# Reading three quarters of w_in once and copying them on chip, with an earlier request for x's third quarter

## The chip, the cores and the metric

One core of one Trainium2 chip. The metric is the device time of one execution in microseconds (us). Executions of one kernel agree within about 0.3%, so a change of 1 us (0.14%) can be seen only in several rounds beside the kernel before.

## The reference, cut to what matters

A causal depthwise convolution over 7 positions with softmax weights, then a two-layer product with leaky ReLU:

```python
w = softmax(weight)                       # 8 heads x 7
out[b, s, ch] = sum_k w[head(ch), k] * x_pad[b, s + k, ch]   # x: 8 x 4096 x 192
h = out.reshape(32768, 192) @ w_in        # w_in: 192 x 2048
g = maximum(0.01 * h, h)
result = g @ w_out                        # w_out: 2048 x 192
```

## The kernel before

Work runs in groups of two batch rows by 256 or 512 positions. The two rows sit in the two partition halves (0 to 63 and 64 to 127), so each half needs its own copy of w_in. A group of 256 positions has eight *steps*: step u multiplies w_in's columns (PSUM tile `ph`, two buffers; PSUM is the memory that TensorE writes), and ScalarE evicts it, that is, copies it out, through leaky ReLU into `g`. Steps 1 and 2 use the first quarter of w_in's columns, steps 3 and 4 the second quarter, and so on. The second product (`po`) of a group runs a group later, interleaved with the first product of the next. Group 0 has nothing to interleave, so it is the start of the pipeline.

```python
def load_first(q, after=None):            # x of the first two blocks, four quarters, SyncE
    t = stage_pool.tile([128, 2, HS, D], FP32, name="x_nat")     # 2 buffers
    for e in range(2):
        ins = nc.sync.dma_start(out=t[:, e, :, :], in_=x[e, q*HT:(q+1)*HT, :]...)
        if after is not None and e == 0:
            tc.add_manual_dep(ins.ins, after.ins.name, ..., reason="leave the DMA engines to w_in")
...
for q in range(WQ):                       # WQ = 4; both halves are read from memory, cast to bf16
    for e in range(2):
        fs = slice(q * F // WQ, (q + 1) * F // WQ)
        nc.gpsimd.dma_start(out=w_in[e*CH:(e+1)*CH, :, fs], in_=moe_w_in[:, fs]...)
nc.gpsimd.dma_start(out=w_out, in_=moe_w_out...)
...
load_first(2, low)                        # low: a ScalarE instruction of the setup
...                                       # conv of group 0 on TensorE (2 chunks) and VectorE (1)
load_first(3); load_x(2); transpose_x(2)
...
def mm1(grp, u):                          # one step
    ph = psum_h.tile([128, 2, ST], FP32, name="ph", tag="ph")
    ...  for c in range(NCH): for e in range(2):
             nc.tensor.matmul(out=ph[:, e, ...], lhsT=w_in[ps, c, f*128:(f+1)*128], rhs=y[ps, c, ...])
    nc.scalar.activation(out=g[blk][...], in_=ph..., func=Prelu, alpha=0.01)
...
# in group 0 (i == 0), after step u (counted from 0):
#   u == 1: transpose_first(1), evac_first(1) on VectorE
#   u == 2: cast_first(2, e) on ScalarE       u == 4: transpose_first(2); evacs[0](act_scale)
#   u in (3, 5): 28 conv matmuls of group 1 each
#   after u == 7: evac_first(2), four conv steps ("early"), evacs[1], all on VectorE
# in group 1: transpose_first(3), later evac_first(3) on VectorE
```

## Time and profile before

| | before |
|---|---|
| time, median | 698.46 us (698.27 to 698.76) |
| span of the profiled run | 696.4 us |
| TensorE busy, share of the chain | 99%, 97% |
| steady stage (both products alternate) starts | about 24 us |

The steady stage is the same in all kernels here: from one fixed point of it, the start of group 1's steps 7 and 8, to the end there are 664.8 to 665.5 us in each of the traces. So that start time is a ruler for the whole span; I call it the ruler step. In the kernel before it is 31.22 us. The lines below are TensorE's order in time: start, length, line and operation, and in brackets its idle time and who ended it.

```profile
13.14 1.75 PE L356 MATMUL ph<-yt,w_in 64*128 64x256 bf16 x24 [0.28 <-ACT g L363]
14.82 1.72 PE L201 MATMUL acc<-xt,diag 64*64 64x256 bf16 x28
20.90 1.48 PE L356 MATMUL ph<-yt,w_in 64*128 64x256 bf16 x24
31.22 1.49 PE L356 MATMUL ph<-yt,w_in 64*128 64x256 bf16 x24
```

Steps 3 and 4 start at 13.14 us, 28 conv matmuls at 14.82, steps 7 and 8 at 20.90 us, and the ruler step at 31.22.

### The profile page before, as it was taken

The page shows a single profiled execution, that of the slowest core. Times are in us where ns is not written, and L with a number is a line of the kernel's source. Part 1 is how long each engine was busy: PE and PEld are TensorE (multiplying, and loading weights), DVE is VectorE, ACT ScalarE, POOL GpSimd, SP SyncE. Part 2 cuts the span into 40 slices and gives each one's busy share as a digit, 9 for nine tenths or more (in the row PEclk, how much of TensorE's full clock was granted, in tenths as well). Part 3 has the DMA queues.
Part 4 walks back from the last instruction along what each step waited for, and adds up shares of the span by engine and source line. Part 5 has one row for each costly group of instructions (what it writes and reads, how often), then busy time and mean ns, then how long its engine had stood idle before and what let it go on. Part 6 is the DMA issues. An engine that isn't in the chain of part 4 may idle for free.

```text
span 696.4 us, 26058 instructions
## 1 busy us (share of the span) xinstructions
PE 689.5 (99%) x11786; PEld 612.7 (88%) x11786; DVE 538.2 (77%) x991; ACT 513.3 (74%) x579; POOL 142.1 (20%) x198
## 2 busy tenths in 40 slices
PE   8999999999999999999999999999999999999997
PEld 6899999678888888888888888888888888888887
DVE  6899999768777788777787777787777787777712
ACT  6888888977777777777777777777777777777770
POOL 6342221320122220222220222211222220000000
PEclk9999999999999999999999999999999999999999
DMA  9986553853556545556545556645556644122112
GB/s 173 127 98 76 82 80 77 88 78 73 76 65 92 82 70 81 74 66 93 81 69 81 73 69 93 79 67 85 66 76 88 86 71 72 53 52 59 47 37 69
DMA packets 184847, 54.39 MB, mean 78 GB/s; under 512 B 148384, under 2 KB 184736, under 8 KB 184736
## 3 DMA queue, kind: packets, MB, share of 16 engines
q0 software_dynamic: 98768, 14.17, 29.7%
q1 hardware_dynamic: 85968, 38.56, 23.1%
q8 instruction: 92, 1.51, 0.9%
q14 instruction: 19, 0.16, 0.1%
HBM read 29.88 MB, written 25.17 MB: 79 GB/s over the span
## 4 chain that ended last, share of the span: by engine, by line
PE 97%; DMA 1%; ACT 1%; POOL 0%; issue 0%; DVE 0%; SPq 0%; POOLq 0%; ACTq 0%
PE po L376 49%; PE ph L356 47%; DMA x_nat<-in_x_dram 1%; ACT g L363 1%; PE acc L201 0%; PE wps L268 0%; ACT diag L296 0%; POOL sel L228 0%; PE warm L250 0%; PE ptr L143 0%; ACT x_bf L128 0%; ACT xt L157 0%; POOL sel L226 0%; DVE o_sb L415 0%; POOL ident masks.py:199 0%
## 5 line engine op out<-in xcount | busy, mean ns | idle before, releaser
L363 ACT ACTIVATE g<-ph 128x1024 bf16<-128x1024 f32 x512 | 496.5, 1021 | 161.0 <-PE ph L356 161.0
L182 DVE SCALAR_TENSOR_TENSOR yt<-xt,wk,yt 128x512 bf16<-128x512 bf16 (+1 forms) x642 | 439.7, 685 | 17.4
L376 PE MATMUL po<-w_out,g 64*128 64x192 bf16 (+1 forms) x8048 | 398.1, 243 | 0.1
L376 PEld LDWEIGHTS <-g 64*128 64x128 bf16 (+1 forms) x8048 | 372.2, 94 | 28.8 <-ACT g L363 0.4
L356 PE MATMUL ph<-yt,w_in 64*128 64x512 bf16 (+1 forms) x3552 | 391.8, 347 | 1.6 <-ACT g L363 1.3
L356 PEld LDWEIGHTS <-w_in 64*128 64x128 bf16 x3552 | 249.9, 94 | 46.1 <-issue 5.0
L79 POOL DMA_DIRECT2D x_bf<-in_x_dram x180 | 133.7, 773 | 431.0 <-DMA xt<-x_bf 422.9
L415 DVE COPY o_sb<-po 128x192 f32<-128x192 f32 x216 | 77.2, 358 | 129.5 <-PE po L376 127.2
L176 DVE TENSOR_SCALAR yt<-xt,wk 128x512 bf16<-128x512 bf16 (+1 forms) x107 | 35.9, 336 | 1.0 <-DMA xt<-x_bf 0.8
L415 ACT COPY o_sb<-po 128x192 f32<-128x192 f32 x40 | 13.1, 327 | 0.0
L201 PE MATMUL acc<-xt,diag 64*64 64x256 bf16 x112 | 7.3, 280 | 0.0
L201 PEld LDWEIGHTS <-diag 64*64 64x64 bf16 x112 | 6.0, 111 | 1.2 <-issue 0.6
L250 PE MATMUL warm<-zero 128*128 128x256 bf16 x20 | 4.5, 373 | 1.1 <-DVE junk L218 1.1
L128 ACT CAST x_bf<-x_nat 128x384 bf16<-128x384 f32 x5 | 2.5, 507 | 3.6 <-DMA x_nat<-in_x_dram 3.6
L238 POOL DMA_DIRECT2D w_in<-in_moe_w_in_dram x8 | 5.1, 643 | 0.0
L157 DVE COPY xt<-ptr 128x384 bf16<-128x384 bf16 x7 | 2.2, 352 | 2.8 <-PE ptr L143 2.8
L250 PEld LDWEIGHTS <-zero 128*128 128x128 bf16 x20 | 2.0, 122 | 2.2 <-DVE junk L218 1.1
L296 ACT ACTIVATE diag<-ident,wkl 128x64 bf16<-128x64 bf16 x14 | 3.6, 339 | 0.0
L128 DVE CAST x_bf<-x_nat 128x384 bf16<-128x384 f32 x3 | 1.2, 439 | 1.4 <-DMA x_nat<-in_x_dram 1.4
L317 ACT ACTIVATE yt<-acc,rsum 128x256 bf16<-128x256 f32 x3 | 1.4, 470 | 1.2 <-PE acc L201 1.2
L143 PEld LDWEIGHTS <-x_bf 64*128 64x128 bf16 x48 | 1.2, 101 | 1.0 <-ACT x_bf L128 1.0
L268 PEld LDWEIGHTS wps<-w,sel 8*128 8x128 f32 x6 | 1.4, 322 | 0.7 <-POOL sel L228 0.7
(28 smaller groups left out, 12.5 us busy)
## 6 DMA issues: line engine op xcount, KB each, us to landing
out_dram<-o_sb SPq DMA_DIRECT2D x128, 192.0 KB, 2.1
x_bf<-in_x_dram POOLq DMA_DIRECT2D x180, 64.0 KB, 3.3
x_nat<-in_x_dram SPq DMA_DIRECT2D x8, 192.0 KB, 5.8
w_in<-in_moe_w_in_dram POOLq DMA_DIRECT2D x8, 192.0 KB, 7.8
xt<-x_bf SPq DMA_TRANSPOSE x90, 2.5
w_out<-in_moe_w_out_dram POOLq DMA_DIRECT2D x1, 768.0 KB, 14.2
w<-in_weight_dram SPq DMA_DIRECT2D x1, 0.2 KB
```

Of the source, the lines that this page charges most:

```text
L79: nc.gpsimd.dma_start(out=t[:, c, :, e, :], in_=src[2 * rp + e, :, :, c * CH : (c + 1) * CH],)
L128: copy(out=x_bf[q // 2][:, :, h * HS : (h + 1) * HS, e, :], in_=x_nat[q][:, e, :, :].rearrange("p s (c k) -> p c s k", c=NCH),)
L176: lambda s=src, d=dst, c=c: nc.vector.tensor_scalar_mul(d, s, wk[:, c, 0:1])
L182: lambda s=src, d=dst, c=c, k=k: nc.vector.scalar_tensor_tensor(out=d, in0=s, scalar=wk[:, c, k : k + 1], in1=d, op0=mybir.AluOpType.mult, ...
L201: lambda k=k, p=p, a=a, e=e, ps=ps: nc.tensor.matmul(out=acc[ps, :T], lhsT=diag[c][ps, p, k, :], rhs=xt[0][ps, c, a : a + T], start=(k == ...
L238: nc.gpsimd.dma_start(out=w_in[e * CH : (e + 1) * CH, :, fs], in_=moe_w_in[:, fs].rearrange("(c p) f -> p c f", p=CH),)
L250: nc.tensor.matmul(out=wa[:, 0, 0:HT], lhsT=zero[:, 0:128], rhs=zero, start=True, stop=True)
L296: act = nc.scalar.activation(out=diag[c][:, 1, k, :], in_=ident2, func=mybir.ActivationFunctionType.Copy, scale=wkl[:, c, k : k + 1],)
L356: nc.tensor.matmul(out=ph[:, e, i * T : (i + 1) * T], lhsT=w_in[ps, c, f * 128 : (f + 1) * 128], rhs=y[ps, c, t0 : t0 + T], start=(c == 0) ...
L363: act = nc.scalar.activation(out=g[blk][:, nf * u : nf * (u + 1), :, t0 : t0 + T], in_=ph.rearrange("p e (i t) -> p i e t", i=nf), func=my ...
L376: ins = nc.tensor.matmul(out=po[m], lhsT=g[b][ps, fc, e, s * 128 : (s + 1) * 128], rhs=w_out[ps, fc, :], start=(rt != 1 and fc == 0), stop ...
L415: copy(out=o_sb[:, n % 2, :], in_=po.pop(n))
```

## The change

The intent: read w_in's last three quarters once instead of twice, copy them to the other partition half by on-chip transfers, and so free the DMA engines for x's third quarter, which loses its artificial wait. The request for w_out stands in the source after the copies, that of block 2's x inside group 1. Some warm-up matmuls go, and one conv eviction moves from ScalarE to VectorE. The core of the diff, cuts marked:

```diff
-    def load_first(q, after=None):
+    def load_first(q):
...                                     (the manual dependence goes)
-    for q in range(WQ):
-        for e in range(2):
...
-    nc.gpsimd.dma_start(out=w_out, in_=moe_w_out.rearrange("(c p) d -> p c d", p=128))
+    fq = [slice(q * F // WQ, (q + 1) * F // WQ) for q in range(WQ)]
+    for q, e in [(0, 0), (0, 1)] + [(q, 0) for q in range(1, WQ)]:
+        nc.gpsimd.dma_start(
+            out=w_in[e * CH : (e + 1) * CH, :, fq[q]],
+            in_=moe_w_in[:, fq[q]].rearrange("(c p) f -> p c f", p=CH),
+        )
...                                     (wkh and wkl shrink to the chunks that use them)
+    load_first(2)
+    for q in range(1, WQ):
+        nc.sync.dma_start(out=w_in[CH:128, :, fq[q]], in_=w_in[0:CH, :, fq[q]])
+    w_out = const_pool.tile([128, NFC, D], BF16)
+    nc.gpsimd.dma_start(out=w_out, in_=moe_w_out.rearrange("(c p) d -> p c d", p=128))
...
-    load_first(2, low)
...
-        warm(3)                        (after each conv chunk of group 0)
...
-    load_x(2)
-    transpose_x(2)
...
-                    evacs[0](act_scale)
...
+                evacs[0](nc.vector.tensor_scalar_mul)
...
+            if i == 1 and j == 1:
+                load_x(2)
+            if i == 2 and j == 1:
+                transpose_x(2)
```

More of the change, by code (lines that the diff above doesn't have):

```diff
@@ L103, in new_xt @@
         nc.vector.memset(xt[rp][:, :, 0:HALO], 0.0)
-    def load_first(q, after=None):
+    def load_first(q):
         t = stage_pool.tile([128, 2, HS, D], FP32, name="x_nat")
         for e in range(2):
-            ins = nc.sync.dma_start(
+            nc.sync.dma_start(
                 out=t[:, e, :, :],
@@ L113, in load_first @@
             )
-            if after is not None and e == 0:
-                tc.add_manual_dep(
-                    ins.ins, after.ins.name,
-                    mybir.DependencyInfo(
-                        mybir.DependencyClass.Sync, mybir.DependencyReason.DATA
-                    ),
-                    reason="leave the DMA engines to w_in",
-                )
         x_nat[q] = t
@@ L234 @@
     w_in = const_pool.tile([128, NCH, F], BF16)
-    for q in range(WQ):
-        for e in range(2):
-            fs = slice(q * F // WQ, (q + 1) * F // WQ)
-            nc.gpsimd.dma_start(
-                out=w_in[e * CH : (e + 1) * CH, :, fs],
-                in_=moe_w_in[:, fs].rearrange("(c p) f -> p c f", p=CH),
-            )
-    w_out = const_pool.tile([128, NFC, D], BF16)
-    nc.gpsimd.dma_start(out=w_out, in_=moe_w_out.rearrange("(c p) d -> p c d", p=128))
+    fq = [slice(q * F // WQ, (q + 1) * F // WQ) for q in range(WQ)]
[4 more added lines that the diff above has]
+        )
     wa = psum_h.tile([128, 2, ST], FP32, name="warm", tag="ph")
@@ L278 @@
     wraw = wps[:, 0, 0 : NCH * (K + 1)].rearrange("p (c k) -> p c k", c=NCH)
-    wkh = const_pool.tile([128, NCH, K], BF16, name="wkh")
-    wkl = const_pool.tile([128, NCH, K], FP32, name="wkl")
-    nc.vector.tensor_copy(out=wkh, in_=wraw[:, :, 0:K])
-    nc.vector.tensor_sub(wkl, wraw[:, :, 0:K], wkh)
+    wkh = const_pool.tile([128, NPEC, K], BF16, name="wkh")
+    wkl = const_pool.tile([128, NPEC, K], FP32, name="wkl")
+    nc.vector.tensor_copy(out=wkh, in_=wraw[:, 0:NPEC, 0:K])
+    nc.vector.tensor_sub(wkl, wraw[:, 0:NPEC, 0:K], wkh)
+    rsum = const_pool.tile([128, NCH, 1], FP32)
+    wk = const_pool.tile([128, NCH, K], FP32, name="wk")
     diag = [const_pool.tile([128, 2, K, CH], BF16, name=f"diag{c}") for c in range(NPEC)]
@@ L295, in diag_low @@
         for k in ks:
-            act = nc.scalar.activation(
+            nc.scalar.activation(
                 out=diag[c][:, 1, k, :], in_=ident2,
@@ L299, in diag_low @@
             )
-        return act
     transpose_first(0)
@@ L306 @@
     evac_first(0, nc.vector.tensor_copy, nc.scalar.copy)
-    low = diag_low(0, range(2, K))
+    diag_low(0, range(2, K))
     diag_high(1)
     diag_low(1, range(K))
-    rsum = const_pool.tile([128, NCH, 1], FP32)
     nc.vector.tensor_scalar_add(rsum, wraw[:, :, K : K + 1], 1e-9)
     nc.vector.reciprocal(rsum, rsum)
-    wk = const_pool.tile([128, NCH, K], FP32, name="wk")
     nc.vector.tensor_mul(wk, wraw[:, :, 0:K], rsum.to_broadcast([128, NCH, K]))
+    load_first(2)
[3 more added lines that the diff above has]
+    nc.gpsimd.dma_start(out=w_out, in_=moe_w_out.rearrange("(c p) d -> p c d", p=128))
     def act_scale(out, in_, scale):
@@ L328 @@
         evac_y(act_scale)
-        warm(3)
     cast_first(1, 0, nc.vector.tensor_copy)
```

## The prediction

> **What bounds the kernel now.** I read the page first, then the chain of waits over the first 26 us, then the order of instructions on TensorE and ScalarE there, then the DMA queues in short windows. The page says who owns the span:
>
> ```profile
> PE 689.5 (99%) x11786; PEld 612.7 (88%) x11786; DVE 538.2 (77%) x991; ACT 513.3 (74%) x579; POOL 142.1 (20%) x198
> PE 97%; DMA 1%; ACT 1%; POOL 0%; issue 0%; DVE 0%; SPq 0%; POOLq 0%; ACTq 0%
> ```
>
> The chain is 97% TensorE, and the 1% that is DMA (some 7 to 9 us) stands in one place. The chain in order of time shows where:
>
> ```profile
> 8.02 8.96 DMA x_nat<-in_x_dram
> 16.98 0.02 issue
> 17.00 0.51 ACT x_bf L128
> 17.51 0.93 ACT g L363
> 18.44 0.04 issue
> 18.48 0.83 PE ph L356 x12
> 19.32 1.65 PE acc L201 x28
> 20.97 0.78 PE ph L356 x12
> 21.75 0.02 issue
> 21.77 1.95 ACT g L363 x2
> 23.72 0.04 issue
> 23.76 0.83 PE ph L356 x12
> 24.59 1.14 PE po L376 x14
> ```
>
> The third quarter of x (x_nat, requested at 7.61 and 8.02 us) takes 8.96 us to land. ScalarE, which works in order, stands before its cast with the leaky-relu evictions of group 0 behind it, and TensorE runs out of free ph banks. From 24.4 us on both products alternate and TensorE never stops: a step of 24 ph and 32 po matmuls each 2.63 us. The change touches nothing after that except one transpose, so only the time at which that stage begins can move. How much idle time is there to win:
>
> ```profile
> 12.00:24.31 12.31, 10.56 (x189) 8.50 (x185) 9.30 (x23) 9.52 (x12) 4.30 (x7) 1.00 1.53 207
> 24.31:34.70 10.39, 10.39 (x210) 10.14 (x207) 9.75 (x23) 8.40 (x12) 4.84 (x8) 1.00 1.26 87
> ```
>
> After the length, the second number is TensorE: 12.31 - 10.56 = 1.75 us idle before the steady stage, none in it. The most that perfect transfers could give is near 1.75 us, 0.25% of 698.46.
>
> **What the queues look like.** The share of the two queues between 8 and 10 us, and from 10 to 12 us (packets, MB, share of 16 engines):
>
> ```profile
> q0 software_dynamic: 333, 0.32, 107.6%
> q1 hardware_dynamic: 2, 0.00, 0.1%
> ...
> q0 software_dynamic: 387, 0.36, 114.0%
> q1 hardware_dynamic: 38, 0.03, 5.7%
> ```
>
> x_nat was requested at 7.61 us by SyncE on q1, yet q1 moves nothing until about 11.5 us. An output store on idle queues has its first packet 0.89 us after its request and has landed after 2.0 us. So 3 us of the delay come from GpSimd's queue: at 94 ns for one of its 1 KB casting packets that is about 32 packets an engine. I choose the reading that a newly arriving q1 transfer first waits for some 32 packets per engine that q0 has already queued; once running, the two alternate (from 12 to 16 us q0 moves 560 packets, q1 516).
>
> The eight w_in loads, requested from 2.90 to 7.98 us, land one by one at 9.0, 10.1, 11.05, 12.3, 13.7, 15.9, 17.2 and 18.6 us; alone on the engines each takes some 1.1 us. None of them holds TensorE today: the quarters are complete at 10.1, 12.3, 15.9 and 18.6 us and first used at 11.1, 13.1, 16.5 and 20.9 us.
>
> **What the Trainium skill says.** "DMA: Bandwidth & Descriptors", section "Issuing engines are not separate DMA queues": transfers of SyncE, ScalarE and GpSimd run on the same 16 DMA engines and interleave. The trace agrees from 12 us on, but the 3 us of silence at 8.5 to 11.5 us is more than fair interleaving. The same page, section "Two DMAs through the same engine are not ordered": a transfer that reads what another writes must be issued after that one's semaphore; so each copy costs a second full latency in series. "TensorE: Matmul & The Clock Gate", section "What's actually happening": the clock gate closes after an idle window of about 3.4 us; in this trace the granted clock is 1.00 in every window that I read after the start, with no idle stretch near that long.
>
> **The change part by part.**
>
> Removed: three w_in loads of 192 KB through q0 (3 x 1.1 = 3.3 us of DMA time). Added: three copies of 192 KB on q1, 192 packets of 1 KB, 12 an engine; a 768-byte plain packet takes 48 ns, so I estimate 55 to 60 ns, 0.7 us each alone. DMA time saved: about 1.2 us in all, less than the halved reads suggest.
>
> Moved earlier: the third quarter of x loses its artificial wait and is requested when the buffer's second cast ends, at 5.3 instead of 7.6 us. q1 is still running the second quarter then, so it goes on alternating with w_in: 32 packets an engine, some 9 pairs at about 200 ns until 8.5 us (w_in is slow there, 150 ns a packet), the other 23 at 142 ns: 11.8 us, landed near 12.2 instead of 17.0. ScalarE's wait of 1.57 us and what it passes on are gone. In return w_in pays 32 x 48 ns = 1.5 us: the second half of quarter 0 lands at 10.9, the first half of quarter 1 at 12.3 instead of 11.05 us.
>
> Not moved, in spite of its place in the source: w_out and block 2's x. GpSimd's stream holds nothing else that waits, so w_out is requested right behind the fifth w_in load, at about 6.1 us (2.9 + 5 x 0.63), x from 7.3 us on. They stand in q0 when the copies come.
>
> The copies: SyncE can request the first only when its source has landed, 12.3 us. It waits 0.9 us for its first packet, then for up to 32 packets of q0 (4 of w_in at 95 ns, 28 of w_out at 51 ns: 1.8 us), runs 12 packets alternating with w_out (12 x 0.108 = 1.3 us), and needs 0.4 us to report: 16.6 us. Without the queueing, 14.8 us; unloaded, 14.3 us. The others follow some 1 to 1.5 us apart. So the second half of quarter 1, today there at 12.3 us, becomes the last to arrive. I take 16.0 us.
>
> TensorE from there: group 0's third and fourth ph steps (1.4), 28 conv matmuls (1.72), a step (0.7), 12 transposes (0.36), a step (0.7), 28 conv matmuls (1.65) come to 6.5 us until the seventh step, which today starts at 20.9 us. Break-even is thus a third step at 14.4 us. At 16.0 us the steady stage begins 1.6 us late; every us of start is a us of end.
>
> Small things: two groups of three warm matmuls go (2 x 0.5 us), but the first ph step still needs VectorE's own conv chunk, ended at 10.79 us, and w_in at 10.9, against a start at 11.11: 0.2 us at most, swallowed by the wait that follows. One ScalarE eviction (0.48 us) becomes a VectorE one (0.48 us). Smaller wkh and wkl: nothing. Sum: +1.6 us, less a little for the chance that I see the queue too dark: 698.46 + 1.4 = 699.9 us.
>
> **The rivals.** (1) The intended gain: copies land soon, x_nat no longer stalls, the third step starts at 13.1 to 13.5 us. Then -1 to -1.5 us, 697.0 to 697.5. For it: ScalarE's wait is real and the page shows the DMA engines full. Against: the source lands no earlier than 11.05 us and an idle-queue transfer takes 2.0 us. (2) Copies wait longer: SyncE stands on each landing in order, 17 us or more; TensorE then idles over 3.4 us from 12.6 us and may lose its clock for a window. Then +2.5 to +4, 701 to 702.5. (3) The bound moves on to w_out (near 23.5 us in both; needed 24.3 today), which caps any gain at about 1 us. (4) xt of block 2: its transposes move from 24.6 us to the middle of group 2, about 40 to 42 us, the first landing some 2.4 us later. VectorE begins that conv at 40.2 us today, TensorE needs its result at 54.8 us and the conv takes 10.1 us: a margin of 2 to 3 us. Late by more, it would add 1 us or two.
>
> **Range and chances.** Rival 1 gives the lower edge, rival 2 the upper: 697.2 to 702.2. A change of 2% is 14 us, while the whole start before the steady stage lasts 24: within 2% is near certain.
>
> **What would show it.** Right: the w_out request at about 6 us; x_nat's third quarter landed near 12 us and no ScalarE wait on it; the copies landing at 15 to 17 us; a TensorE gap after the transposes at 12.5 us, ended by a copy; the seventh step at 21.5 to 23 us; an unchanged 2.63 us step after that. Wrong: the first copy landed before 14 us (then faster), w_out requested only after the copies, a granted clock under 1.00, or VectorE's wait for block 2 reaching TensorE near 55 us.

## The result, and the profile after

The changed kernel took 704.58 us (median of 4, 704.07 to 705.42), the kernel before beside it 698.37 us. The ratio is 1.0089, 95% interval 1.0072 to 1.0107: 6.2 us longer, within 2% but clear of noise, and outside the predicted range of 697.2 to 702.2 us. (A ratio is the mean time of one kernel's fast runs over that of the other's of the same rounds, so not quite the ratio of the medians.) Executions over 1.5% slower than the fastest of the same kernel are left out of the means.

The chain of waits of the changed kernel, start and length in us:

```profile
11.86 6.35 DMA w_in<-w_in
18.21 0.05 issue
18.26 2.74 PE ph L348 x23
```

The DMA that the chain waits for is no longer x but the first copy. It is requested at 11.86 us, as soon as its source has landed, and lands 6.35 us later. Steps 3 and 4 wait for it. At full clock they take 1.48 us (e6 below), here 2.74. TensorE's order in time shows the same, and what follows:

```profile
18.26 2.74 PE L348 MATMUL ph<-yt,w_in 64*128 64x256 bf16 x23 [4.14 <-DMA w_in<-w_in]
20.93 3.02 PE L193 MATMUL acc<-xt,diag 64*64 64x256 bf16 x28
27.13 1.48 PE L348 MATMUL ph<-yt,w_in 64*128 64x256 bf16 x24
36.77 1.50 PE L368 MATMUL po<-w_out,g 64*128 64x192 bf16 x32 [0.54 <-DVE xt L149]
38.09 1.49 PE L348 MATMUL ph<-yt,w_in 64*128 64x256 bf16 x24
```

The 28 conv matmuls take 3.02 us instead of 1.72. Step 7 starts at 27.13 us instead of 20.90; the ruler step at 38.09 instead of 31.22, 6.87 us later, and the spans differ by 6.8 us (703.2 and 696.4). Nothing is lost after that: from 40 to 120 us TensorE is busy throughout, although VectorE waits 2.8 us for block 2's transposed x at 49.87 us.

Why work after the gap runs at half pace is in the windows of busy time. Columns: window, its length, TensorE busy (instructions), weight loads, VectorE, ScalarE, GpSimd, then the granted TensorE clock, DMA share and GB/s. The edges are those of the recorded clock changes:

```profile
13.41:16.82 3.41, 0.43 (x12) 0.05 (x4) 3.02 (x8) 1.31 (x2) 1.48 (x2) 1.00 1.51 209
16.82:20.24 3.42, 1.98 (x20) 1.46 (x22) 0.85 (x2) 0.49 (x1) 0.00 (x0) 0.50 1.60 226
20.24:23.65 3.41, 3.41 (x33) 2.52 (x31) 0.00 (x0) 2.27 (x4) 0.99 (x2) 0.50 1.71 206
```

In one window of 3.41 us TensorE worked 0.43 us. At its end the clock fell to 0.50 and stayed there for 6.83 us: the next window, busy 1.98 us of 3.42, did not bring it back; the one after, fully busy, did, and from 23.65 us on it is 1.00 again. It is not one trace's accident: the mean clock of all four executions is 0.994 or 0.995, which is what 6.83 us at half clock make of some 703 us; in e1 and e3 to e9 below every execution has 0.999 or 1.000.

What did the copy do for 6.35 us? The queues of the changed kernel from 15 to 16 us and from 16 to 17 us (packets, MB, share of 16 engines). q1 is SyncE's queue, q0 GpSimd's:

```profile
q0 software_dynamic: 500, 0.19, 163.4%
q1 hardware_dynamic: 1, 0.00, 0.1%
...
q0 software_dynamic: 257, 0.10, 80.2%
q1 hardware_dynamic: 147, 0.15, 54.2%
```

The copy's packets (1 KB each) start only after 16 us, by the trace's packet records at 16.09, 4.2 us after the request; the one packet of q1 from 15 to 16 us is a 4-byte one that ends x's transfer. Until then q0 moves w_out, which GpSimd had requested at 6.12 us: in its stream of work nothing stood before that request that had to wait, whatever the order in the source.

### The profile page after: what moved, and what is told of

The parts are those of the page before. It is cut to its first block, busy times and chain, and to the rows that moved or that the text cites. A ratio compares the mean times of both kernels' runs of the same rounds, so it can differ in the third digit from the quotient of the medians.

```text
span 703.2 us, 26045 instructions
## 1 busy us (share of the span) xinstructions
PE 692.1 (98%) x11780; PEld 614.2 (87%) x11780; DVE 538.6 (77%) x992; ACT 513.3 (73%) x578; POOL 140.1 (20%) x195
## 4 chain that ended last, share of the span: by engine, by line
PE 95%; DMA 2%; DVE 2%; POOL 0%; issue 0%; ACT 0%; POOLq 0%; ACTq 0%
PE po L368 48%; PE ph L348 46%; DVE yt L174 1%; DMA w_in<-in_moe_w_in_dram 1%; DMA w_in<-w_in 1%; PE acc L193 0%; POOL w_in L230 0%; POOL sel L220 0%; DVE yt L168 0%; DVE xt L149 0%; DVE yt L199 0%; ACT g L355 0%; POOL sel L218 0%; DVE o_sb L407 0%; POOL ident masks.py:199 0%
## 5 line engine op out<-in xcount | busy, mean ns | idle before, releaser
L193 PE MATMUL acc<-xt,diag 64*64 64x256 bf16 x112 | 9.7, 345 | 0.0
L193 PEld LDWEIGHTS <-diag 64*64 64x64 bf16 x112 | 7.7, 140 | 2.2 <-issue 0.6
L230 POOL DMA_DIRECT2D w_in<-in_moe_w_in_dram x5 | 3.2, 652 | 0.0
```

What stands on the lines that cost most here:

```text
L193: lambda k=k, p=p, a=a, e=e, ps=ps: nc.tensor.matmul(out=acc[ps, :T], lhsT=diag[c][ps, p, k, :], rhs=xt[0][ps, c, a : a + T], start=(k == ...
L230: nc.gpsimd.dma_start(out=w_in[e * CH : (e + 1) * CH, :, fq[q]], in_=moe_w_in[:, fq[q]].rearrange("(c p) f -> p c f", p=CH),)
```

## The experiments

Theory: the first copy waits behind what GpSimd's queue already holds, so step 3 starts near 18.2 us; the gap then halves the clock. Rivals: on-chip copies are slow in themselves; or another part of the change (the VectorE eviction, the missing warm matmuls, block 2's later x) is the loss. Ten kernels ran, all correct. Times are medians, each beside the kernel before on the same chip.

| run | us | before beside it | ratio (95% interval) |
|---|---|---|---|
| changed kernel | 704.58 | 698.37 | 1.0089 (1.0072 to 1.0107) |
| e1_conv_first | 701.38 | 698.69 | 1.0034 (1.0019 to 1.0049) |
| e2_wout_late | 701.96 | 698.69 | 1.0048 (1.0033 to 1.0063) |
| e3_no_copies | 697.69 | 698.69 | 0.9982 (0.9967 to 0.9997) |
| e4_dve_copy | 699.00 | 698.69 | 1.0005 (0.9988 to 1.0021) |
| e5_before_early_x | 698.35 | 698.77 | 0.9990 (0.9977 to 1.0002) |
| e6_keep_clock | 702.29 | 698.77 | 1.0052 (1.0037 to 1.0068) |
| e7_dve_copy_evac | 697.43 | 698.77 | 0.9981 (0.9969 to 0.9994) |
| e8_conv_first_evac | 700.56 | 698.77 | 1.0023 (1.0010 to 1.0037) |
| e9_dve_copy_order | 696.78 | 698.63 | 0.9974 (0.9960 to 0.9988) |
| e10_copy_on_act | 704.52 | 698.63 | 1.0083 (1.0065 to 1.0102) |

**e3: without the copies.** The edit, on the changed kernel:

```diff
-    for q, e in [(0, 0), (0, 1)] + [(q, 0) for q in range(1, WQ)]:
+    for q, e in [(q, e) for q in range(WQ) for e in range(2)]:
...
-    for q in range(1, WQ):
-        nc.sync.dma_start(out=w_in[CH:128, :, fq[q]], in_=w_in[0:CH, :, fq[q]])
```

> The changed kernel with the three copies taken out and w_in read twice again; all else of the change stays. Theory (the copies are the whole loss): x's third quarter lands 1.5 to 3 us earlier than in the kernel before, w_in 1 to 1.5 us later, nothing idles over 1 us: 697.5 to 699 us, within 1 us of the kernel before. Rival (another part of the change, such as the VectorE eviction or the missing warm matmuls, costs it): 701 us or more.

697.69 us, 1.0 us below the kernel before, with everything else of the change in place. The rival that another part of the change costs the time falls: the copies, in place of the second reads, are the whole loss, and the rest is a small gain. TensorE's longest wait for w_in was 0.24 us, and the ruler step starts at 30.55 us:

```profile
30.55 1.49 PE L346 MATMUL ph<-yt,w_in 64*128 64x256 bf16 x24
```

**e6: keeping the clock up.** In the changed kernel, before step 3 of group 0, into the bank that the step then overwrites:

```diff
+        if grp is groups[0] and u == 2:
+            for _ in range(36):
+                nc.tensor.matmul(
+                    out=ph[:, 0, 0:HT], lhsT=zero[:, 0:128], rhs=zero, start=True, stop=True
+                )
```

> The changed kernel with 36 matmuls on zeros in the gap before the third step of group 0, 3.9 us at full clock, written to a bank that the step overwrites. Nothing else is changed, so the copy lands at 18 us as before. Theory (the half clock after the gap is 2 to 2.6 us of the loss): the clock stays at 1.00, the third step still starts near 18.3 us, the seventh near 24.7 instead of 27.1: 701.5 to 702.7 us, 2 to 3 us faster than the changed kernel. Rival (the lower clock is only a mark of the idle time and costs nothing of its own): no faster than the changed kernel, 704 us or more.

TensorE's order in time:

```profile
13.56 4.09 PE L345 MATMUL ph<-zero 128*128 128x256 bf16 x36 [0.28 <-ACT g L360]
18.03 1.48 PE L353 MATMUL ph<-yt,w_in 64*128 64x256 bf16 x23 [0.17 <-DMA w_in<-w_in]
24.34 1.48 PE L353 MATMUL ph<-yt,w_in 64*128 64x256 bf16 x24
35.02 1.49 PE L353 MATMUL ph<-yt,w_in 64*128 64x256 bf16 x24
```

The copy is as late as ever (step 3 at 18.03 us), but steps 3 and 4 take 1.48 us and step 7 starts at 24.34 us. 702.29 us, 3.5 us over the kernel before instead of 6.2: useless matmuls saved about 2.7 us. So the half clock costs 2.7 us, and the lateness of the copies the other part. (The intervals of the two ratios do not overlap, but each is some 2 us wide, so by the times alone this split is good to 1 or 2 us.) The two traces agree: the ruler step is at 35.02 us here and 38.09 us in the changed kernel.

**e2: w_out really after the copies.**

```diff
-        nc.sync.dma_start(out=w_in[CH:128, :, fq[q]], in_=w_in[0:CH, :, fq[q]])
+        last_copy = nc.sync.dma_start(out=w_in[CH:128, :, fq[q]], in_=w_in[0:CH, :, fq[q]])
...
+    tc.add_manual_dep(late.ins, last_copy.ins.name, ..., reason="w_out after the copies")
```

> The changed kernel, but w_out (and with it block 2's and 3's x) is requested only after the third copy has landed, as the words of the change say. Theory (the copy stands behind what GpSimd's queue already holds): first packet of the first copy within 1.5 to 2 us of its request instead of 4.1, landed 2.5 to 3.5 us after it (14.5 to 15.5 us) instead of 6.35; no clock drop; w_out then lands near 23 to 25 us and may hold the first po matmul; 698.5 to 700 us. Rival (a copy from one half of the on-chip memory to the other is itself slow): the first copy still takes 5 us or more, and with w_out later still the time is above the changed kernel's 704.6 us.

The queues from 13 to 14 us, and the time from request to landing (least, median, most) of the first and the third copy, first of this run, then of the changed kernel. The view pairs no landing with the second copy; by its semaphore, the counter that a transfer raises when it lands, that one took 3.6 and 6.2 us:

```profile
q1 hardware_dynamic: 145, 0.13, 51.6%
q0 software_dynamic: 85, 0.08, 46.0%
```

```profile
DMA to landing us min/median/max: 3.1/3.7/4.3
```

```profile
DMA to landing us min/median/max: 6.4/6.6/6.9
```

Of q1's 145 packets 93 are the copy's (1 KB); the others end x's third quarter. The first moves at 13.35 us by the packet records, 1.4 us after the request at 11.97, instead of 4.2 us: the queueing is shown. The copy lands after 4.3 us instead of 6.35. That is slower than I had expected (2.5 to 3.5). The semaphore records say where the excess lies: 15 of its 16 increments had come by 15.19 us, 3.2 us after the request, and the last at 16.27. What held that one is not shown. The quickest copy, the third, took 3.1 us, with GpSimd's queue empty but the second copy still on its own queue. So the rival is partly right: no copy was a matter of 2 us. The expectation "no clock drop" was a miss too. The gap here was only 2.56 us (from 13.75 to 16.31 us), and the clock fell all the same:

```profile
12.66:16.07 3.41, 0.81 (x21) 0.43 (x15) 2.67 (x7) 1.69 (x2) 0.00 (x0) 1.00 0.80 179
16.07:19.49 3.42, 3.18 (x29) 2.05 (x31) 1.15 (x3) 1.68 (x3) 1.45 (x2) 0.50 0.61 166
```

The window before the drop had 0.81 us of work in 3.41. 701.96 us in all, where 698.5 to 700 had been expected. w_out, landed at 26.05 us, held no matmul.

**e10: the first copy on ScalarE's queue.**

```diff
-    for q in range(1, WQ):
+    for q in range(2, WQ):
         nc.sync.dma_start(out=w_in[CH:128, :, fq[q]], in_=w_in[0:CH, :, fq[q]])
...
+    nc.scalar.dma_start(out=w_in[CH:128, :, fq[1]], in_=w_in[0:CH, :, fq[1]])
     cast_first(1, 0, nc.vector.tensor_copy)
```

> The changed kernel with the first copy requested on ScalarE's own queue instead of SyncE's. Theory (the copy waits for packets that GpSimd's queue already holds, whichever queue it is on): first packets again some 3 us later than an idle queue would have them, near 15.5 to 16 us, landed 17.5 to 18.3; 703.5 to 705 us. Rival (it waits behind the tail of x's third quarter on SyncE's queue): first packets near 13 us, landed by 15.5; 699.5 to 701 us.

Requested at 11.35 us on a queue of its own (q10 in the records). The queues from 15 to 16 us:

```profile
q0 software_dynamic: 399, 0.15, 127.7%
q10 hardware_dynamic: 64, 0.07, 23.6%
```

q10 moves nothing from 14 to 15 us and its first packet at 15.58 us, 4.2 us after the request as before, although x's tail on q1 had landed by 14.43 us. The copy landed at 17.44 us. 704.52 us (two executions), as the changed kernel. So the copy does not wait behind SyncE's own queue; with e2, it waits for GpSimd's.

**e1: conv matmuls into the gap.** At the place after step 2, all 56 conv matmuls of group 1 instead of 28 after step 4 and 28 after step 6:

```diff
                     per = len(ahead)
+                    for job in pe_ahead:
+                        job()
+                    pe_ahead = []
```

> The changed kernel with all 56 conv matmuls of the next half group moved ahead of the third step of group 0, into the gap. Theory (first copy lands near 18.2 us and holds the third step; the 4.1 us gap then halves the clock until 23.65 us): the copy still lands at 18 us, but the gap after it is under 1 us, the clock stays at 1.00, and the seventh step starts near 21.5 us instead of 27.1: 4.5 to 6 us faster than the changed kernel, 698.7 to 700 us. Rival (VectorE's later conv and evictions are what is late): no more than 1 us faster than the changed kernel.

The clock stayed at 1.00, and step 3 again started at 18.19 us. The thinnest window, of the same length, had 2.04 us of work:

```profile
14.91:18.33 3.42, 2.04 (x37) 1.65 (x33) 1.71 (x4) 0.00 (x0) 0.74 (x1) 1.00 1.45 226
```

701.38 us: 3.2 us faster than the changed kernel, not the 4.5 to 6 expected. By the trace two things took the rest; only the second was tested (e8). With the conv matmuls gone from between the steps, the steps run into ScalarE's evictions of some 1 us each (four waits of 0.20 to 0.57 us). And a new wait appears, on a VectorE eviction that frees a PSUM bank for po:

```profile
33.16 1.50 PE L368 MATMUL po<-w_out,g 64*128 64x192 bf16 x32 [1.17 <-DVE xt L149]
```

**e8: the same, with that eviction earlier.**

```diff
             if i == 1 and j == 1:
                 transpose_first(3)
+                evac_first(3, nc.vector.tensor_copy, nc.vector.tensor_copy)
...
-            if i == 1 and j == 3:
-                evac_first(3, nc.vector.tensor_copy, nc.vector.tensor_copy)
```

> The earlier run with the conv matmuls in the gap, and the same move of the last eviction. Theory: its wait of 1.17 us for that eviction is gone, 0.8 to 1.2 us faster than that run (701.4): 700.0 to 700.8 us. What stays over the kernel before is then the late third step, with the evictions of ScalarE in series behind it. Rival as in the run with VectorE copies: less than 0.4 us faster.

700.56 us, 0.8 us faster than e1, and the wait is gone. It was real and only a matter of VectorE's order. (The intervals of e1 and e8 overlap, as do those of e4 and e7, and of e7 and e9: that each wait went is shown by the traces, and the times agree with it.)

**e4: the copies on VectorE.** On the changed kernel, no copies by transfer, but:

```diff
     cast_first(1, 1, nc.vector.tensor_copy)
+    nc.vector.tensor_copy(out=w_in[CH:128, :, fq[1]], in_=w_in[0:CH, :, fq[1]])
...
                     evac_first(1, nc.vector.tensor_copy, nc.vector.tensor_copy)
+                    for q in (2, 3):
+                        nc.vector.tensor_copy(
+                            out=w_in[CH:128, :, fq[q]], in_=w_in[0:CH, :, fq[q]]
+                        )
```

> The changed kernel with the three copies made by VectorE instead of by transfers, the first right after its casts, the other two after the evictions that follow. Theory (it is the second transfer in series behind a full queue that costs): a copy takes about 0.5 us, the third step starts at 13 to 13.6 us, no clock drop; VectorE's conv starts some 1.5 us later, which has slack: 696.5 to 698 us, faster than both kernels. Rival (any dependence of the second half on the first costs as much): 700 us or more.

Step 3 starts at 13.64 us: the dependence of one half on the other costs nothing when the copy is quick. But 699.00 us missed the forecast, because what was won was given back at the same eviction as in e1, later in VectorE's line by the time of the copies:

```profile
30.89 1.50 PE L367 MATMUL po<-w_out,g 64*128 64x192 bf16 x32 [1.55 <-DVE xt L149]
```

**e7: the same, with evac_first(3) earlier** (the edit of e8).

> The copies on VectorE as in the earlier run, and the last eviction of transposed x moved ahead of seven conv steps on VectorE. Theory (there the wait of 1.55 us of a po matmul for that eviction ate what the copies won): the wait is gone, 1.2 to 1.6 us faster than the earlier run with VectorE copies (699.0): 697.2 to 698 us, faster than both kernels. Rival (VectorE's conv is itself the bound, the eviction only its mark): less than 0.5 us faster, and TensorE waits for yt at the start of the next group.

697.43 us, as expected. In its profiled run w_in's last quarter landed late (16.09 us), VectorE stood waiting for it, and a conv eviction behind it kept TensorE:

```profile
23.66 1.38 PE L347 MATMUL ph<-yt,w_in 64*128 64x256 bf16 x22 [1.03 <-DVE yt L199]
```

**e9: VectorE's order mended.** The third copy moves behind VectorE's conv (to u == 2), and evacs[1] ahead of the four early conv steps:

```diff
                         cast_first(2, e, nc.scalar.copy)
+                    nc.vector.tensor_copy(out=w_in[CH:128, :, fq[3]], in_=w_in[0:CH, :, fq[3]])
...
                 evacs[0](nc.vector.tensor_scalar_mul)
+                evacs[1](nc.vector.tensor_scalar_mul)
...
-                evacs[1](nc.vector.tensor_scalar_mul)
```

> The run with VectorE copies and the early eviction, with two orders of VectorE mended: the third copy goes behind the conv steps, and the second conv eviction ahead of four conv steps of the following block. In that run TensorE waited 1.03 us for this eviction. Theory (it is only the order of VectorE's work that is left): the wait is gone, 0.7 to 1.1 us faster than 697.4: 696.3 to 696.9 us, below both kernels. Rival (w_out, landed near 21.8 us, or ScalarE's evictions take the wait's place): within 0.4 us of 697.4.

696.78 us, ratio 0.9974, the fastest seen; it beats both kernels. The copy itself, in the list of this line's instructions:

```profile
L324 DVE COPY w_in<-w_in x1: 685/685/685, 12.0 to 12.0; 64x1536 bf16<-64x1536 bf16 x1
```

0.685 us, against 6.35 us by transfer, and 3.1 us for the quickest transfer (e2). Against e3 (0.9982) and e7 (0.9981) the intervals overlap and the runs were not side by side, so I do not claim that it is the best of the three.

**e5: the kernel before with the early request alone.** `load_first(2, low)` becomes `load_first(2)`.

> The kernel before with one part of the change alone: the artificial wait of x's third quarter is taken away. Theory (that request is the useful part of the change): x's third quarter lands near 13.5 to 15.5 us instead of 17.0, the ScalarE wait of 1.57 us is gone, w_in lands 1 to 1.5 us later: 0.3 to 1.3 us faster than before, like the run without copies (697.7). Rival (the gain of that run came from the removed warm matmuls or the later request of block 2's x): within 0.3 us of the kernel before, or slower.

698.35 us, 0.42 us below, with an interval that holds 1: in the expected direction, but inconclusive. The trace shows the ScalarE wait gone and the ruler step at 30.82 us instead of 31.22, after 0.31 us given back at evac_first(3). What e3 has over this run (the missing warm matmuls, the VectorE eviction, block 2's x) was not tried piece by piece.

## Why the prediction was wrong

Right were the reading of the bound, the early request of w_out (6.12 us; 6.1 predicted), the mechanism (the copies become the last to arrive, a wait in series behind GpSimd's queue), and the conversion from step 3 to the end. That conversion put break-even at a third step at 14.4 us; e6, where step 3 starts at 18.03 us, gives 18.03 - 14.4 = 3.6 us, and 3.5 us was measured; that they agree so closely is luck, since e6's interval is 2.6 to 4.8 us. Rival 4 did not happen: VectorE waited for block 2's x, TensorE did not.

Two terms of the sum were wrong: the wait of the first copy was too short, and half clock had no place in it.

1. *The landing of the first copy.* "I take 16.0 us" became 18.21. (The terms written add up to 16.7, not 16.6, and 16.0 was taken without a reason.) Its source landed as predicted (11.84; 12.3 predicted). The wait behind q0 had been put at 1.8 us after the 0.9 us of an idle queue, from a count of 32 packets an engine, of which most would be short w_out ones. It was 3.3 us (16.09 - 11.86 - 0.9), about the 3.0 us that x had waited behind the longer w_in packets in the kernel before. Running and reporting took 2.1 us (16.09 to 18.21) instead of 1.7. The same count failed for x's third quarter: I let it run on beside w_in without a wait and land near 12.2 us; it was requested at 4.89 us, moved nothing until 9.2 us, and its second half landed at 15.38 us. That one cost nothing. A fixed number of packets is not the rule: between request and first packet q0 moved 43 packets an engine in the kernel before (x), but 93 in the changed kernel and 88 in e10 (the copy), while the time was 3.9, 4.2 and 4.2 us and the bytes 40, 43 and 42 KB an engine. What sets it stays open: behind the lighter x loads of the steady stage an output store had its first packet after 1.2 us.
2. *The clock.* Rival 2 named it, priced lateness and clock together at +2.5 to +4, gave it no share of the central sum, and set the upper edge of the range by it. It is what happened. The gap of the changed kernel (4.14 us) did pass the 3.4 us that rival 2 named. The price is simple to work out: at half clock TensorE was busy for 5.4 us (1.98 + 3.41), which at full clock would have been half as long: 2.7 us lost, which is what e6 measured. The prediction also relied on what the Trainium skill, "TensorE: Matmul & The Clock Gate", section "What's actually happening", says of an idle window of about 3.4 us. It took a *gap* of that length to be needed. The windows are of that length here too (3.41 us), but a nearly empty window was enough: e2 lost its clock with a gap of 2.56 us. And e2 prices the case that the central sum had in mind: step 3 at 16.31 us instead of 16.0 cost 3.3 us (701.96 against 698.69), not 1.4. By the prediction's own break-even 1.9 us of that is lateness; half of the 3.18 us that TensorE worked at half clock, 1.6 us, is about the rest.

The sum as measured, by medians against each run's own kernel before: the rest of the change -1.0 us (e3); lateness of the copies +4.5 us (from e3 at -1.0 to e6 at +3.5); half clock +2.7 us (from e6 to the changed kernel at +6.2). By the ruler step of the profiled runs: -0.67, +4.47 and +3.07, together 6.87 us; the last of these holds 0.3 us of the wait for evac_first(3) (0.54 against 0.25 us) and 0.2 us of a later step 3 (18.26 against 18.03). One trace alone is uncertain by some tenths: full clock was first granted between 7.4 and 10.0 us in these runs, and the first conv runs slower until then.

So the expected gain was there, and about 1 us in size. It was lost because a saving of bytes was bought with a second transfer in series behind a full queue. The DMA engines' busy share said nothing of that.

## What to carry to other kernels

A transfer that depends on another transfer pays a full latency again (3.1 us at the least here), plus, here, 3.3 us behind the backlog of GpSimd's queue, whichever queue it was issued on (e10); order in the source does not hold back a queue that has nothing to wait for. Price the clock when a change can leave TensorE nearly idle for one window: the gap and the slow windows after it are two separate losses, and filling the gap with matmuls, even useless ones (e6), saves the second. When data need only cross partitions, an idle compute engine did it in a ninth of the time (under a quarter of the quickest transfer's), but its line of work, done in order, then has to be looked through for evictions that now come late.

## What the Trainium skill lacked or had wrong

- "TensorE: Matmul & The Clock Gate", section "What's actually happening": it ties the half clock to an idle window of about 3.4 us, and no page says how much work a window may hold and still count as idle. Here a window with 0.43 us of work (changed kernel) and one with 0.81 us (e2, gap 2.56 us) ended in half clock; one with 2.04 us (e1) did not. A window with 1.98 us of work at half clock did not restore it; ones with 3.18 and 3.41 us did.
- "DMA: Bandwidth & Descriptors", section "Queues, rings and completion order": it has the engines take turns between queues packet by packet. No page gives the delay seen here: a transfer newly requested on SyncE's or ScalarE's queue moved its first packets 4.2 us after the request, against 0.9 us on idle queues, while GpSimd's queue went on with some 450 to 500 packets per us (changed kernel, e10).
- No page has a time for a small copy between the partition halves: 192 KB took 3.1 us from request to landing at best (e2), 6.35 us behind w_out, and 0.685 us on VectorE.
